# Four small row loads of an attention stage issued from ScalarE's queue instead of SyncE's

## The chip, the cores and the metric

The kernel runs on one core of a Trainium2 chip. The metric is the time of one execution on the device in microseconds (us). The five engines of the core run side by side, each through its own list of instructions in order: TensorE (PE; its weight loads are shown as PEld), VectorE (DVE), ScalarE (ACT), GpSimd (POOL) and SyncE (SP). SP issues nearly all transfers (DMA); ACT can issue transfers too, between its own instructions.

## The reference

Attention over 4 batches of 8 heads, with a causal mask and a bias from the running sum of `s`; its output goes through two gated MLPs (called MoE).

```python
# q, k, v: (4, 8, 576, 64), s: (4, 8, 576)
scores = (1 / sqrt(64)) * q @ k.T
cum = cumsum(maximum(s, 0), axis=-1)
bias = -(cum[:, :, :, None] - cum[:, :, None, :])
scores = where(causal, -1e9, scores + minimum(bias, 0))
attn = softmax(scores)
x = (attn @ v) as (2304 tokens, 512)
x = rmsnorm(x) * rms_g
x = (silu(x @ w_gate) * (x @ w_val)) @ w_out      # d_ff 1536
x = (silu(x @ w2_gate) * (x @ w2_val)) @ w2_out   # d_ff 1536
```

## The kernel before

The tokens of a batch are cut into group A (queries 0 to 255) and group B (256 to 575). Groups A of batches 0 and 1 are computed first, in a cheaper way, while the first weights still come in: these are the 16 *early heads*, called here head 0 to head 15 in their order (0 to 7 are batch 0, 8 to 15 batch 1; class `EarlyUnit`, function `attend_early`). After them, the norm of group A of batch 0 (`normalise`) and the first gate and value matmuls of the MoE (`moe1`, L1086) run; the later attention heads lie between those.

For an early head the scores are one matmul per query tile (`scores`, L899; two tiles: "first" and "second" scores), in float32, with 128 rows to contract: 64 of q and k, and one row more, row `D`, that holds 1 on the q side and the cumulated s on the k side, so that the matmul adds the cumulated s. The rest is zero. Both sides lie in a tile `lq` (two tiles, `lq_117` and `lq_121`, each with two halves, so head n uses the place of head n - 4). DVE adds the mask and finds the extremum of a row (L690), ACT takes the exponential (L701), PE transposes it (L917), ACT or DVE copies the result out (`pTA`, L922 or L923), PE multiplies with v (L927, the "values"), and ACT or DVE copies into `x` (L932 or L933). The squares of `x` for the norm are summed by tiny matmuls (L965, 128x2). The first step on PE from the norm towards the MoE is a transpose at L1058; L1066 and L1086 follow.

The method `load` issues an early head's transfers: q and k (L879, 128 KB), for heads 4 to 15 the row of the cumulated s (L884, `lq<-cumA`, 1 KB, from a tile in SBUF to row `D` of `lq`), and v (L891, 64 KB; for the first four heads from ACT, L888). The weights of the first MLP are loaded in pieces of 512 KB (L434, `raw<-in_w_gv`); ACT and DVE and POOL turn them into two float32r parts (L438 to L449).

What stands where is set by a planner (`Plan`): every piece of work is told to it with an engine, an estimated duration and a priority (`pri`, the lower the sooner), and it plays the engines against an inner clock and writes their lists in the order that comes out. For a transfer, SP's entry is free for the next after 450 ns at least, while what reads the data is due some 2.3 us later; `later` is a further delay that it adds between what the transfer waits for and its issue. Work of an early head has priority n on the compute engines, its transfers n - 1000. On the chip the lists are fixed, and semaphores make each instruction wait for what it needs. The transfers take eight semaphores (DMAHW0 to DMAHW7) in turn, and each waits until the transfer before it on its own semaphore has landed.

Of the kernel before, what the change touches and what calls it, by code (L numbers as in the profile page):

```python
# [22 lines left out]
NB, NH, S, D = 4, 8, 576, 64  # L23
# [17 lines left out]
PE, DVE, ACT, POOL, SP, NONE = "PE", "DVE", "ACT", "POOL", "SP", "NONE"  # L41
# [38 lines left out]
class Plan:  # L80
# [20 lines left out]
    def op(self, eng, ns, fn, r=(), w=(), pri=0.0, later=0, port=False, slow=0.0):  # L101

        n = len(self.ops)
        done = 0
        if eng == SP:  # L110
            took = ns / self.RATE
            ns = max(450.0, took)
            done = 2300.0 + took - ns + slow
        deps, shared = set(), []
        for accesses, writes in ((r, False), (w, True)):
            for a in accesses:
                buf, part = a if isinstance(a, tuple) else (a, None)
                key = buf if isinstance(buf, str) else buf.key
                live = self.live.setdefault(key, [])
                keep = []  # L120
                for part2, m, wrote in live:
                    meets = part is None or part2 is None or part == part2
                    if meets and (writes or wrote) and m != n:
                        deps.add(m)
                    if not (writes and meets and (part is None or part == part2)):
                        keep.append((part2, m, wrote))
                keep.append((part, n, writes))
                self.live[key] = keep
                if not isinstance(buf, str) and buf.share is not None and buf not in shared:
                    shared.append(buf)  # L130
                    buf.uses += 1
        engs = eng if isinstance(eng, list) else [(eng, ns)]
        self.ops.append((engs, fn, deps, pri, done, shared, later, port))
        return n
# [166 lines left out]
def tile_kernel(  # L301
# [16 lines left out]
    op = plan.op  # L318
# [10 lines left out]
    def buf(pool, tag, shape, dtype, name=None):  # L329
        return Buf(f"{pool}.{tag}",  # L330
                   lambda: pools[pool][1].tile(shape, dtype, name=name or tag, tag=tag))
# [143 lines left out]
    cumA = buf("at", "pTB1", [P, 2 * P], F32, "cumA")  # L475
# [100 lines left out]
    class Head:  # L576
# [13 lines left out]
        def load(self, pri):  # L590
            b, h, n, nv = self.b, self.h, self.n, self.nv
            i = b * NH + h
            c0 = self.c0
            q0, k0, c0_ = lq_parts(self.ql, 0)
            q1, k1, c1_ = lq_parts(self.ql, 1)
            self.qp, self.kp = [k0, k1], [q0, q1, c0_, c1_]
            op(SP, 4 * P * n, lambda en: en.dma_start(
                out=self.ql()[:, :n], in_=qk[b, h, :, 1, :n]), w=self.kp, pri=pri, later=2500)
            op(SP, 4 * D * (QW - c0), lambda en: en.dma_start(
                out=self.ql()[:D, S + c0:], in_=qk[b, h, :D, 0, c0:]),  # L600
               w=self.qp, pri=pri, later=2500)
            op(SP, 4 * P * n, lambda en: en.dma_start(
                out=self.cb()[:, :n], in_=cum_d[i:i + 1, :n].to_broadcast([P, n])),
               r=["cum_d"], w=[self.cb], pri=pri, later=2500)
            op(SP, 256 * P * nv, lambda en: en.dma_start(out=self.vl()[:, :nv], in_=vp[b, h, :, :nv]),
               w=[self.vl], pri=pri, later=2500)
# [241 lines left out]
    class EarlyUnit(Unit):  # L848
# [28 lines left out]
        def load(self, pri):  # L877
            ql, i = self.ql
            op(SP, 8 * D * 256, lambda en: en.dma_start(  # L879
                out=ql()[0:D, :, 288 * i:288 * i + 256], in_=qk[self.b, self.h, 0:D, :, 0:256]),  # L880
               w=self.parts[:2], pri=pri)
            n = self.b * NH + self.h
            if not self.first:
                op(SP, 1024, lambda en: en.dma_start(  # L884
                    out=ql()[D:D + 1, 1, 288 * i:288 * i + 256], in_=cumA()[n:n + 1]),
                   r=[cumA, self.rows], w=self.parts[2:], pri=pri, later=1000)
            if self.first:
                op(ACT, 450, lambda en: en.dma_start(  # L888
                    out=self.v(), in_=vp[self.b, self.h, :, 0:2]), w=[self.vl], pri=pri - 1e6)
            else:  # L890
                op(SP, 512 * P, lambda en: en.dma_start(  # L891
                    out=self.v(), in_=vp[self.b, self.h, :, 0:2]), w=[self.vl], pri=pri)
# [241 lines left out]
    later = setup()  # L1134
# [767 lines left out]
```

## Time and profile before

| | us |
|---|---|
| median of 3 timed runs (lowest, highest) | 1055.18 (1053.97, 1057.35) |
| the profiled execution | 1057.39 |
| its span, first to last instruction of the program | 1055.6 |
| PE busy in the span | 1040.2 (99%) |
| DVE, ACT, POOL busy | 771.7, 641.5, 273.5 |
| mean granted clock of PE, share of full speed | 0.997 |

The profiled execution's own time is 1.8 us more than its span: that lies before the first and after the last instruction. A busy PE in the profile says that matmuls are under way, and not at which rate; the granted clock, at one of two levels (1.00 is 2.4 GHz, 0.50 is 1.2 GHz), is told for each stretch.

### The profile page before, as it was taken

What the parts mean: (1) busy time and instruction counts of PE and PEld (TensorE: products, weight loads), DVE (VectorE), ACT (ScalarE), POOL (GpSimd) and SP (SyncE); (2) the same over time, 40 slices, a digit from 0 to 9 for tenths busy, and PEclk for the clock granted to TensorE, in tenths of its full rate; (3) what the DMA queues carried; (4) which work ended last, traced back from release to release, by engine and by line L of the source; (5) the groups of instructions that cost most, each with busy time, mean ns of one, the idle gap of its engine ahead of it and who ended that gap; (6) DMA issues with size and microseconds to landing.
All of it is one profiled execution on the core that took longest, in us unless ns stands there. A gap on an engine that the chain in (4) does not pass through costs nothing.

```text
span 1055.6 us, 19496 instructions
## 1 busy us (share of the span) xinstructions
PE 1040.2 (99%) x6322; PEld 937.2 (89%) x6322; DVE 771.7 (73%) x1880; ACT 641.5 (61%) x1373; POOL 273.5 (26%) x370
## 2 busy tenths in 40 slices
PE   8899999999999999999999999999999999999998
PEld 6599999999999999999988889888888888888888
DVE  7699788777777776757779887665667766976462
ACT  6689778867664775333466865555556444665652
POOL 4368556544343542000000000212122221300000
PEclk9899999999999999999999999999999999999999
DMA  7797555534546732666697662666667667888673
GB/s 204 229 282 221 144 150 148 164 117 128 158 142 204 246 106 85 188 208 206 206 299 244 197 222 84 222 210 220 228 202 256 219 232 263 292 259 261 207 244 105
DMA packets 127959, 211.17 MB, mean 200 GB/s; under 512 B 16176, under 2 KB 55600, under 8 KB 127856
## 3 DMA queue, kind: packets, MB, share of 16 engines
q1 hardware_dynamic: 126656, 209.32, 62.8%
q8 instruction: 50, 0.82, 0.3%
q10 hardware_dynamic: 1200, 0.60, 0.2%
q14 instruction: 53, 0.43, 0.1%
HBM read 145.29 MB, written 64.56 MB: 199 GB/s over the span
## 4 chain that ended last, share of the span: by engine, by line
PE 79%; DMA 7%; DVE 6%; ACT 3%; issue 3%; POOL 1%; SPq 1%; ACTq 0%; POOLq 0%; DVEq 0%
PE mo L1086 21%; PE mo L1455 8%; PE mo L1626 8%; PE sps L1626 6%; PE tp L1455 6%; PE sps L1455 5%; PE tp L745 4%; PE tp L733 3%; PE sps L664 2%; PE mo L1702 2%; DMA raw<-in_w_gv 2%; PE sps L1086 2%; PE tp L1086 2%; PE mo L1510 2%; DMA lq<-cumA 1%
## 5 line engine op out<-in xcount | busy, mean ns | idle before, releaser
L1086 PE MATMUL mo<-xL,H 128*128 128x256 f32 (+1 forms) x672 | 201.8, 300 | 0.1
L1086 PE MATMUL mo<-xH,H 128*128 128x256 f32 (+1 forms) x672 | 200.7, 300 | 0.3
L1086 PE MATMUL mo<-xH,L 128*128 128x256 f32 (+1 forms) x672 | 200.2, 298 | 0.0
L1351 DVE TENSOR_TENSOR hL<-hh,hH 128x512 fp32r<-128x512 f32 (+1 forms) x192 | 125.2, 662 | 67.1 <-ACT hH L1348 66.4
L1348 ACT ACTIVATE hH<-hh 128x512 fp32r<-128x512 f32 (+1 forms) x192 | 115.2, 603 | 91.6 <-DVE hL L1351 21.3
L1086 PEld LDWEIGHTS mo<-xL,H 128*128 128x128 f32 x672 | 127.0, 189 | 1.0 <-POOL xL L1075 0.5
L1086 PEld LDWEIGHTS mo<-xH,H 128*128 128x128 f32 x672 | 126.7, 189 | 1.1 <-ACT xH L1073 0.6
L1086 PEld LDWEIGHTS mo<-xH,L 128*128 128x128 f32 x672 | 126.9, 189 | 0.2
L701 ACT ACTIVATE sc<-sc,col 128x128 f32<-128x128 f32 (+3 forms) x128 | 73.2, 572 | 48.4 <-DVE col L690 46.1
L1455 PE MATMUL mo<-hH,wo 128*128 128x512 f32 x312 | 97.8, 389 | 0.0
L1455 PEld LDWEIGHTS mo<-hH,wo 128*128 128x128 f32 x312 | 58.6, 188 | 12.2
L1455 PE MATMUL mo<-hL,wo 128*128 128x512 f32 x156 | 61.1, 391 | 0.2 <-DVE hL L1351 0.2
L1455 PE MATMUL tp<-hH,wo 128*128 128x512 f32 x192 | 60.4, 389 | 0.0
L1093 ACT ACTIVATE t<-mo 128x256 f32<-128x256 f32 (+1 forms) x84 | 33.9, 403 | 43.4 <-PE mo L1086 43.3
L1632 ACT ACTIVATE u<-sps 128x512 f32<-128x512 f32 x48 | 28.5, 593 | 50.6 <-PE sps L1626 48.8
L745 PE MATMUL tp<-pTB,vst 128*128 128x320 f32 (+2 forms) x320 | 52.2, 294 | 1.6 <-ACT pTB L736 1.0
L1455 PE MATMUL sps<-hH,wo 128*128 128x512 f32 x168 | 52.9, 389 | 0.0
L1095 DVE SCALAR_TENSOR_TENSOR t<-t,mo 128x256 f32<-128x256 f32 (+1 forms) x84 | 37.8, 450 | 19.4 <-ACT t L1093 19.1
L738 DVE TENSOR_TENSOR pTB<-tp,pTB 128x512 fp32r<-128x512 f32 x64 | 44.0, 687 | 8.3 <-ACT pTB L736 7.2
L745 PEld LDWEIGHTS tp<-pTB,vst 128*128 128x128 f32 x320 | 46.5, 189 | 3.6 <-ACT pTB L736 1.7
L1589 POOL TENSOR_TENSOR tmp<-x,x 128x512 f32<-128x512 f32 x2 | 2.9, 1454 | 178.5 <-DVE x L1471 178.5
L733 PE MATMUL tp<-ident,sc 128*128 128x128 f32 x304 | 46.9, 274 | 0.6 <-DVE x L754 0.4
(289 smaller groups left out, 2925.9 us busy)
## 6 DMA issues: line engine op xcount, KB each, us to landing
raw<-in_w_gv SPq DMA_DIRECT2D x44, 511.8 KB, 5.4
tb<-h_d SPq DMA_DIRECT2D x48, 256.0 KB, 3.9
t<-tb SPq DMA_DIRECT2D x48, 256.0 KB, 2.4
hh<-t SPq DMA_DIRECT2D x48, 256.0 KB, 3.1
lq<-in_qk SPq DMA_DIRECT2D x32, 288.0 KB, 3.6
cb<-cum_d SPq DMA_DIRECT2D x32, 288.0 KB, 3.9
hh<-h_d SPq DMA_DIRECT2D x36, 256.0 KB, 3.6
h_d<-hh SPq DMA_DIRECT2D x54, 128.0 KB, 2.3
```

Of the source, the lines that this page charges most:

```text
L701: op(ACT, c_act(o + m, 2) + 35, lambda en: en.activation(sc()[:m, :o + m], sc()[:m, :o + m], ACTF.Exp, scale=-1.0, bias=col()[:m, 0, t:t + 1],
L733: op(PE, C_TR, lambda en, pt=pt, a=a, kb=kb, t=t: en.transpose(pt()[:, a * P:a * P + P], self.sc[t]()[:, kb * P:kb * P + P], ident()), r=[ ...
L738: op(DVE, c_tt(n), lambda en, pt=pt, c=c: en.tensor_tensor(out=place(L, c), in0=source(pt, c), in1=f32(place(H, c)), op=ALU.subtract), r=[ ...
L745: op(PE, c_mm(n), lambda en, w=w, z=z, kb=kb, d0=d0, n=n, o=o: en.matmul(po()[:, o:o + n], vst[j]()[:, kb, :], pT[g][z]()[:, d0:d0 + n], s ...
L1086: op(PE, c_mm(n), lambda en, a=a, x=x, c=c, k=k, i=i: en.matmul(ps()[:, :n], a()[:, c], x()[:, k, :n], start=(k == 0 and i == 0), stop=(k ...
L1093: op(ACT, c_act(n), lambda en: en.activation(t()[:, :n], gp()[:, :n], ACTF.Tanh, scale=0.5), r=[gp], w=[t], pri=pri)
L1095: op(DVE, c_tt(n), lambda en: en.scalar_tensor_tensor(out=t()[:, :n], in0=t()[:, :n], scalar=1.0, in1=gp()[:, :n], op0=ALU.add, op1=ALU.mu ...
L1348: op(ACT, c_act(n) + 35, lambda en: en.activation(H(), src(), ACTF.Copy), r=[src, *after], w=[H], pri=pri)
L1351: lambda en: en.tensor_tensor(out=L(), in0=src(), in1=f32(H()), op=ALU.subtract),
L1455: op(PE, c_mm(n), lambda en, m=m, w=w, xx=xx, kk=kk, i=i: en.matmul(ps[m]()[:, :n], w(), xx(), start=first and kk == 0 and i == 0, stop=kk ...
L1626: op(PE, c_mm(n), lambda en, w=w, xx=xx, cut=cut, kk=kk, i=i: en.matmul(ps()[:, :n], W[w]()[:, cut], xx(), start=first and kk == 0 and i == 0,
L1632: op(ACT, c_act(n), lambda en: en.activation(dst(), ps()[:, :n], ACTF.Copy), r=[ps], w=[dst], pri=-1.0e4)
```

## The change

For heads 12 to 15, the row of the cumulated s is issued from ACT's queue and not from SP's. The planner is told 450 ns on ACT, the delay `later` of 1000 is taken out, and the priority of the issue is n - 3 among ACT's other work (n - 1000 before, on SP). Heads 4 to 11 keep their rows on SP. What is transferred stays the same.

```diff
             n = self.b * NH + self.h
             if not self.first:
-                op(SP, 1024, lambda en: en.dma_start(
+                late = self.i >= 2 * NH - 4
+                op(ACT if late else SP, 450 if late else 1024, lambda en: en.dma_start(
                     out=ql()[D:D + 1, 1, 288 * i:288 * i + 256], in_=cumA()[n:n + 1]),
-                   r=[cumA, self.rows], w=self.parts[2:], pri=pri, later=1000)
+                   r=[cumA, self.rows], w=self.parts[2:], pri=pri + 997 if late else pri,
+                   later=0 if late else 1000)
```

Since the planner orders all engines together, the lists differ from there on. The lines behind the edit shift by two: L899 becomes L901, L891 L893, and so on.

On SP, before: the list from the q and k of head 12 on to the q and k of head 14. `lq1_121` holds the odd heads, `lq0_117` the even ones; `raw` is a weight load, `vl` a v load (heads 10, 11 and 12 here); the semaphores that an entry waits for stand in brackets.

```order
L879 DMA lq0_117<-in_qk 64x2x256 [waits DMAHW6_49,PE_49]
L891 DMA vl0_126<-in_vp 128x128 [waits DMAHW7_49,PE_49]
L884 DMA lq0_117<-cumA_114 1x16x16 [waits DMAHW0_49]
L434 DMA raw0_455<-in_w_gv 128x2047 [waits DMAHW1_49]
L891 DMA vl1_136<-in_vp 128x128 [waits DMAHW2_49,PE_49]
L434 DMA raw1_479<-in_w_gv 128x2047 [waits DMAHW3_49]
L879 DMA lq1_121<-in_qk 64x2x256 [waits DMAHW4_49]
L891 DMA vl0_126<-in_vp 128x128 [waits DMAHW5_49,PE_49]
L884 DMA lq1_121<-cumA_114 1x16x16 [waits DMAHW6_49]
L879 DMA lq0_117<-in_qk 64x2x256 [waits DMAHW7_49]
```

The same place on SP now.

```order
L879 DMA lq0_117<-in_qk 64x2x256 [waits DMAHW0_49,PE_49]
L893 DMA vl0_126<-in_vp 128x128 [waits DMAHW1_49,PE_49]
L434 DMA raw0_451<-in_w_gv 128x2047 [waits DMAHW2_49]
L434 DMA raw1_470<-in_w_gv 128x2047 [waits DMAHW3_49]
L893 DMA vl1_136<-in_vp 128x128 [waits DMAHW6_49,PE_49]
L879 DMA lq1_121<-in_qk 64x2x256 [waits DMAHW7_49,DMAHW5_49]
L879 DMA lq0_117<-in_qk 64x2x256 [waits DMAHW0_49,PE_49]
```

The rows are gone from SP, and the second weight load stands one entry sooner; the q and k of head 13 still stand behind both weight loads. The v load of head 10 now waits for DMAHW1.

On ACT, the list now, from the exponential of head 8's second scores on to the copy of head 9's transposes (before, the same list without the four DMA entries, except for numbers).

```order
L701 ACTIVATE sc10_427,tot1_149<-sc10_427,col0_186 128x256 [waits DVE_49]
L885 DMA lq0_117<-cumA_114 1x16x16 [waits DMAHW1_49,PE_49,Pool_49]
L924 ACTIVATE pTA1_260<-tp0_436 128x384 [waits PE_49]
L701 ACTIVATE sc01_449,tot1_149<-sc01_449,col1_201 128x128 [waits DVE_49,Activation_49]
L885 DMA lq1_121<-cumA_114 1x16x16 [waits DMAHW6_49,DMAHW5_49,PE_49]
L438 ACTIVATE cvy_173<-raw1_379 128x512 [waits DMAHW0_49]
L701 ACTIVATE sc11_464,tot1_149<-sc11_464,col1_201 128x256 [waits DVE_49,Activation_49]
L960 ACTIVATE sq1_110<-x0_119 128x256 [waits DVE_49]
L924 ACTIVATE pTA0_223<-tp0_468 128x384 [waits PE_49]
L701 ACTIVATE sc00_478,tot1_149<-sc00_478,col2_217 128x128 [waits DVE_49]
L701 ACTIVATE sc10_485,tot1_149<-sc10_485,col2_217 128x256 [waits DVE_49,Activation_49]
L885 DMA lq0_117<-cumA_114 1x16x16 [waits DMAHW3_49,DMAHW4_49,PE_49,Pool_49]
```

The row of head 12 stands behind head 8's exponential, on the semaphore DMAHW1 that the v load on SP waits for; head 13's follows two entries on, head 14's (the last entry shown) and head 15's, right behind it, stand ahead of the copy of head 9's transposes.

On PE, before: from the second scores of head 12 to the second scores of head 13. The values of head 10 (`tp1_548`) and the transposes of head 11 (`tp0_557`) stand ahead of the first scores of head 13 (`sps0_564`).

```order
L899 MATMUL sps1_537<-lq0_117 128x256
L927 MATMUL tp1_548<-pTA0_223,vl0_126 64x256
L927 MATMUL tp1_548<-pTA0_223,vl0_126 64x128
L917 MATMUL tp0_557<-ident_140,sc01_510 128x128
L917 MATMUL tp0_557<-ident_140,sc11_515 128x128 x2
L899 MATMUL sps0_564<-lq1_121 128x128
L965 MATMUL mo2_569<-half_228,sq0_334 128x2 x2
L899 MATMUL sps1_575<-lq1_121 128x256
```

The same place on PE now.

```order
L901 MATMUL sps1_541<-lq0_117 128x256
L901 MATMUL sps0_551<-lq1_121 128x128
L929 MATMUL tp1_558<-pTA0_223,vl0_126 64x256
L929 MATMUL tp1_558<-pTA0_223,vl0_126 64x128
L919 MATMUL tp0_564<-ident_140,sc01_517 128x128
L919 MATMUL tp0_564<-ident_140,sc11_521 128x128 x2
L901 MATMUL sps1_571<-lq1_121 128x256
```

The first scores of head 13 have moved ahead of head 10's values and head 11's transposes. Some 25 rows further on, the transpose at L1060 (L1058 before) stands behind the values of head 14 and the transposes of head 15, which before stood behind it.

## Rows read from the trace of the kernel before

**Rows 1.** The page, busy us (share of the span) and instructions of each engine.

```profile
PE 1040.2 (99%) x6322; PEld 937.2 (89%) x6322; DVE 771.7 (73%) x1880; ACT 641.5 (61%) x1373; POOL 273.5 (26%) x370
```

**Rows 2.** Stretches: length, busy PE, PEld, DVE, ACT, POOL, granted clock, DMA share, GB/s.

```profile
10.00:20.00 10.00, 8.74 (x52) 6.04 (x50) 7.23 (x29) 8.60 (x26) 4.69 (x8) 1.00 0.64 162
...
20.00:30.00 10.00, 9.90 (x61) 6.94 (x60) 8.48 (x31) 9.15 (x30) 4.78 (x5) 1.00 0.70 186
...
35.83:38.31 2.48, 0.00 (x1) 0.03 (x1) 0.60 (x2) 1.22 (x3) 1.45 (x2) 0.99 0.67 205
38.31:45.00 6.69, 6.69 (x21) 4.47 (x22) 2.67 (x12) 1.98 (x8) 1.94 (x2) 0.50 0.53 153
...
60.00:1040.00 980.00, 975.94 (x5934) 886.52 (x5934) 723.87 (x1714) 595.97 (x1244) 250.24 (x332) 1.00 0.63 201
```

**Rows 3.** Waits of PE, 0 to 60 us: us in total, times, longest.

```profile
PE sps L899 <- DMA lq<-cumA: 3.5, 2, 2.5
```

**Rows 4.** Chain that ended last, 5 to 52 us: start, us, what.

```profile
31.70 6.48 DMA lq<-cumA
```

**Rows 5.** Timeline of PE: start, us, instruction, count, idle before it.

```profile
14.07 0.46 PE L899 MATMUL sps<-lq 128*128 128x128 f32 x2 [1.05 <-DMA lq<-cumA]
...
33.68 0.60 PE L899 MATMUL sps<-lq 128*128 128x256 f32 x2
34.49 0.86 PE L927 MATMUL tp<-pTA,vl 128*64 128x256 f32 x4 [0.21 <-ACT pTA L922]
35.28 0.55 PE L917 MATMUL tp<-ident,sc 128*128 128x128 f32 x3
38.31 0.77 PE L899 MATMUL sps<-lq 128*128 128x128 f32 x2 [2.48 <-DMA lq<-cumA]
```

**Rows 6.** Timeline of SP's queue: start, us, transfer issued.

```profile
25.96 0.54 SPq L879 DMA_DIRECT2D lq<-in_qk  x1
26.60 1.56 SPq L891 DMA_DIRECT2D vl<-in_vp  x1
28.21 0.55 SPq L884 DMA_DIRECT2D lq<-cumA  x1
28.82 0.57 SPq L434 DMA_DIRECT2D raw<-in_w_gv  x1
...
29.91 0.43 SPq L434 DMA_DIRECT2D raw<-in_w_gv  x1
30.38 0.55 SPq L879 DMA_DIRECT2D lq<-in_qk  x1
```

**Rows 7.** Issues near 30.4 and 28.2 us, KB, us to landing; all twelve rows.

```profile
lq<-in_qk SPq DMA_DIRECT2D x1, 128.0 KB, 7.3
...
lq<-cumA SPq DMA_DIRECT2D x1, 1.0 KB, 1.8
...
DMA to landing us min/median/max: 1.7/4.8/7.4
```

**Rows 8.** Timeline of ACT: start, us, instruction, idle before it.

```profile
1.17 2.28 ACTq L888 DMA_DIRECT2D vl<-in_vp  x4
...
26.15 0.19 ACT L701 ACTIVATION_READ_ACCUMULATOR sc<-sc,col 128x1 f32 x1
26.50 0.49 ACT L922 ACTIVATE pTA<-tp 128x384 f32<-128x384 f32 x1 [0.17 <-PE tp L917]
...
31.87 0.49 ACT L922 ACTIVATE pTA<-tp 128x384 f32<-128x384 f32 x1 [0.87 <-PE tp L917]
```

**Rows 9.** Timeline of PE, from head 13's values to the MoE.

```profile
46.68 0.86 PE L927 MATMUL tp<-pTA,vl 128*64 128x256 f32 x4 [0.65 <-DVE pTA L923]
...
48.52 0.38 PE L1058 MATMUL mo<-ident,sq 128*128 128x128 f32 x2
48.83 0.86 PE L927 MATMUL tp<-pTA,vl 128*64 128x256 f32 x4
...
52.31 0.44 PE L917 MATMUL tp<-ident,sc 128*128 128x128 f32 x2 [0.49 <-ACT sc L701]
```

## The prediction

> **What bounds the kernel now.** I read the busy totals first: TensorE (PE) is busy 1040.2 of 1055.6 us [rows 1], so whatever the change is worth must show as PE idle time, or as PE time at the lower clock. The stretches [rows 2] say where that is. From 60 to 1040 us PE stands idle only 980 - 975.94 = 4.06 us; the change's own place, the early heads before 52.6 us, is where PE waits. There the list of PE's waits has one row at its head: the scores matmul waits 3.5 us, in two pieces, the longest 2.5, for `lq<-cumA`, the row of the cumulated s [rows 3]. The timeline of PE shows them: 1.05 us at 14.07 (head 4, which the change leaves alone) and 2.48 us, 35.83 to 38.31, ahead of the scores of head 13 [rows 5]. Right behind the second the granted clock goes to 0.50, the lower level (1.2 GHz), from 38.31 to 45, with PE busy all of the 6.69 us [rows 2]. The same work at the higher level would take half, so the fall costs up to 3.35 us.
>
> The chain of waits names the transfer: the row of head 13 is issued at 31.70 and lands 6.48 us later, at 38.18 [rows 4]; the matmul follows 0.13 us behind. But the same matmul needs head 13's q and k too, and these were issued on the same queue at 30.38 and took 7.3 us [rows 6, 7]: they landed at 37.68. So of the 2.48 us, only the last 0.50 belong to the row; the other 1.98 belong to q/k, which stand behind two weight loads of 512 KB each (28.82 and 29.91) [rows 6].
>
> **The change, term by term.** Times are those of the profiled execution, 1057.39 us in all, of which the span is 1055.6 and 1.8 lies around it. It stands 2.21 us above the median of the three timed runs (1055.18), so the terms are summed first and then put on the median.
>
> *Rows leave SP's queue.* Four issues of 0.55 us go. Only the row of head 12 (28.21) stands ahead of q/k of head 13; the next entry, a weight load, started 0.61 us after it [rows 6]. So q/k come 0.61 us earlier (if nothing new holds SP, below) and land at 37.07. The row of head 13, issued on ACT near 28 us and not at 31.70, lands long before; its 0.50 us is gone. Together: PE resumes 0.50 + 0.61 = 1.11 us earlier, at 37.20. **-1.11.**
>
> At this place a rule speaks against the change. The twelve rows, 1.0 KB each, landed from SP's queue in as little as 1.7 and as much as 7.4 us [rows 7]: what is queued ahead decides, not the size. The Trainium skill ("DMA: Bandwidth & Descriptors", section "Issuing engines are not separate DMA queues") says that transfers issued from several engines share the same 16 DMA engines and that only the time of the issuing sequencer is saved. By that alone the sum would lose the 0.50 and keep the 0.61, which ends at 1055.9. No run here yet shows a small row on ACT's queue next to heavy SP traffic.
>
> *Work that PE now does behind the wait.* The order shows head 13's first scores moved ahead of the values of head 10 and the transposes of head 11. Before, these ran from 34.49 to 35.83 [rows 5], ahead of the wait; now PE comes to the wait that much earlier and has them still to do. **+1.34** (at the higher clock).
>
> *Issues on ACT.* Four issues on ACT took 2.28 us, 0.57 each [rows 8]. ACT is busy 9.15 of 10 us from 20 to 30 us [rows 2], so the first two (heads 12 and 13, near 26.3 and 28 us) push its exponentials and copies back by up to 1.14 us, and PE's transposes and values with them. The other two stand ahead of the copy at 31.87, for which ACT sat idle 0.87 us [rows 8]: they hide, but for 0.27. What covers the delay is PE's wait for q/k of head 13: PE would come to it at 35.83 - 1.34 = 34.49, wait until 37.20, which is 2.71 us, and arriving 1.14 later changes nothing. **0**; without that wait, +1.14 to +1.41.
>
> *The clock.* A wait of 2.71 us is nearest to the one of 2.48 that the fall followed. **0**; -3.35 if the clock holds.
>
> *Up to the MoE.* In 46.0 to 52.6 us PE idled 0.65 and 0.49 us [rows 9]. The order now puts L1060 (before: L1058, 48.52), the first PE step of the way from the norm to the MoE, behind the values of head 14 and the transposes of head 15, which before filled waits on that way: they are worth the same 1.34. Bounds -1.14 (both idles gone) to +1.34; the eight small squares matmuls still fill, so I take **0**.
>
> *Everything later.* The planner orders all engines anew after 28 us. The nearest row for what that can do is the idle of 60 to 1040 us, 4.06: gone, or twice as much. **0**, bounds -4.06 to +4.06.
>
> Sum: -1.11 + 1.34 = +0.23. On the profiled time 1057.6, on the median **1055.4 us**.
>
> **Rivals.**
>
> *The clock holds (faster).* If ACT's issues do delay PE by 1.14, the wait at head 13 is 2.71 - 1.14 = 1.57 us, and that is nearer to the 1.05 at 14.07, behind which the granted clock stayed at 1.00 [rows 2], than to 2.48. Then 1055.4 - 3.35 = 1052.1, a hair from the bound of faster. For it: the arithmetic above. Against it: q/k may well land as late as before, which gives 2.2. And the three timed runs spread from 1053.97 to 1057.35, 3.4 us, as much as the fall costs: some of them may not have had it, and then less is to be gained on the median.
>
> *SP is held by a row on ACT (slower).* The transfers take eight semaphores in turn over both queues, and each waits for the transfer before it on its own. In the new order the v load of head 10 on SP (26.60 before) waits for the semaphore of head 12's row on ACT. ACT reaches that row at 26.33 [rows 8]. With the 1.8 us that this row took before [rows 7] it lands at 28.1, and SP's issue of v lasted until 28.16 anyhow [rows 6]: free. With the median of such rows, 4.8 [rows 7], it lands at 31.13, the weight loads go at 31.5 and not 28.21, and q/k of head 13 come 3.3 us later: 1058.7. It decides for slower (over 1058.35) from a landing of about 4.5 us on. For it: half of the twelve rows on SP took 4.8 us or more. Against it: ACT's queue is empty at that time.
>
> *Only the transfer is earlier.* If PE is held by ACT before the wait anyway, the 1.34 is not lost and only -1.11 remains: 1054.1, no change that counts.
>
> *The later order decides.* 1055.4 - 4.06 = 1051.3, or 1059.5.
>
> **How the numbers follow.** 0.3% is 3.2 us, about what a measurement of this kernel can tell from no change: faster is under 1052.0, slower over 1058.3. The forecast has 0.40 (its own range 1053.5 to 1058.0; 0.37 same, 0.03 slower). The clock holds: 0.28 (0.19 faster with any small gain besides, 0.09 same). SP held: 0.14 (all slower but 0.03). Only the transfer: 0.12, same. Later order: 0.06, half each way. Faster 0.19 + 0.03 = 0.22; slower 0.03 + 0.11 + 0.03 = 0.17; same 0.61. The range is that of the later order's two ends, 1051.3 to 1059.5; it takes in the clock's 1052.1 and SP's 1058.7 and leaves out waits on SP near the longest landing of 7.4.
>
> **What would show it.** Right: PE's wait ahead of the scores of head 13 is put down to `lq<-in_qk`, not to `lq<-cumA`, and still lasts 2 to 3 us, ending near 37.2; the rows on ACT's queue land within some 2 us; a stretch at 0.50 follows. Wrong: no row at 0.50 after 38 us (then the clock's rival); SP's v load of head 10 waits beyond 28.5 us (SP held); the wait of head 13 gone altogether, which would say that q/k were not what stood behind the row; or an idle of PE between 60 and 1040 us that is over a microsecond off 4.06.

## The result and the profile after

The changed kernel took 1065.72 us (median of 6 runs, 1063.97 to 1067.12), the kernel before 1056.05 in the runs beside it (6 runs, 1053.0 to 1057.93): a ratio of 1.0103, 95% interval 1.0085 to 1.0121. It is slower by some 10 us. The forecast was 1055.4, no change, with a range that ended at 1059.5: wrong on both counts.

The profiled execution took 1063.97 us, its span 1062.1, 6.5 more than before. On the page (busy us of each engine) PE did the same number of matmuls in 1.9 us more [rows 1], and stood idle 20.0 us (1062.1 - 1042.1) instead of 15.4; DVE is busy 11.8 us longer, POOL 11.0 us less.

```profile
PE 1042.1 (98%) x6322; PEld 938.0 (88%) x6322; DVE 783.5 (74%) x1887; ACT 644.0 (61%) x1378; POOL 262.5 (25%) x358
```

In the stretches that answer to [rows 2] (length, busy PE, PEld, DVE, ACT, POOL, granted clock, DMA share, GB/s) the 2.48 us in which PE stood still ahead of head 13 are now 1.83 us of work, the stretch at the lower clock behind head 13 is gone and one from 50.31 to 60.55 has come, and from 60 to 1040 us PE idles 980 - 972.07 = 7.93 us instead of 4.06.

```profile
35.83:38.31 2.48, 1.83 (x11) 1.16 (x10) 1.78 (x7) 2.43 (x10) 1.50 (x2) 1.00 1.08 236
50.31:60.55 10.24, 10.10 (x42) 9.14 (x43) 8.78 (x20) 8.01 (x18) 5.49 (x6) 0.50 0.82 233
60.00:1040.00 980.00, 972.07 (x5915) 881.60 (x5915) 734.41 (x1718) 594.98 (x1242) 236.16 (x317) 1.00 0.63 200
```

Where the time went is read from equal stretches of both kernels, PE alone (length, PE busy, granted clock, DMA share, GB/s). Before:

```profile
10.00:20.00 10.00, 8.74 (x52) 1.00 0.64 162
...
30.00:40.00 10.00, 7.31 (x38) 0.91 0.84 244
40.00:50.00 10.00, 9.35 (x40) 0.74 0.70 235
50.00:60.00 10.00, 9.51 (x74) 1.00 0.92 290
60.00:70.00 10.00, 10.00 (x80) 1.00 0.91 290
70.00:80.00 10.00, 9.52 (x74) 1.00 0.94 295
...
100.00:1040.00 940.00, 936.59 (x5628) 1.00 0.63 199
```

After:

```profile
10.00:20.00 10.00, 8.39 (x40) 0.83 0.67 167
...
30.00:40.00 10.00, 8.93 (x50) 1.00 0.89 261
40.00:50.00 10.00, 7.02 (x41) 1.00 0.85 251
50.00:60.00 10.00, 9.61 (x40) 0.52 0.87 249
60.00:70.00 10.00, 8.64 (x64) 0.97 0.95 282
70.00:80.00 10.00, 8.56 (x69) 1.00 1.03 342
...
100.00:1040.00 940.00, 934.88 (x5624) 1.00 0.63 199
160.00:200.00 40.00, 38.51 (x296) 1.00 0.47 137
```

Busy time times granted clock is, roughly, the work that PE did at its full rate. From 30 to 40 us the changed kernel did 2.3 us more of it (8.93 against 7.31 x 0.91 = 6.65): the stall of head 13 is gone, as the change intends. From 40 to 80 us it did 7.02 + 9.61 x 0.52 + 8.64 x 0.97 + 8.56 = 29.0 us, the kernel before 9.35 x 0.74 + 9.51 + 10.00 + 9.52 = 36.0. So 7 us are lost in these 40 us, which the change's rows don't touch. From 100 to 1040 us only 1.7 more are, nearly all of it from 160 to 200 us, where PE idles 1.49 us (0.08 before).

Part of the difference between these two traces has nothing to do with the change. In the changed kernel's trace the clock was at 0.50 from 16.18 to 19.59 us as well, behind a wait of 1.61 us for head 4's row. The lists of both kernels are the same there, and the same product with V starts at 25.12 us before and at 27.19 after: 2.1 of the 6.5 us of span were there before the first moved row was issued. Of the 20 traces of this case seven have a fall between 14 and 21 us, among them s2 and h3, which follow the list of the kernel before there; so it comes and goes from execution to execution.

PE's timeline (start, us, instruction, idle before it) shows what is left of the wait at head 13, a new wait of 2.76 us ahead of head 14's product with V, and the first MoE matmul (L1088) at 54.42.

```profile
37.76 0.46 PE L901 MATMUL sps<-lq 128*128 128x128 f32 x2 [0.65 <-DVE col L690]
...
44.95 0.55 PE L919 MATMUL tp<-ident,sc 128*128 128x128 f32 x3
48.26 0.86 PE L929 MATMUL tp<-pTA,vl 128*64 128x256 f32 x4 [2.76 <-ACT pTA L924]
...
50.25 1.51 PE L929 MATMUL tp<-pTA,vl 128*64 128x256 f32 x4 [0.43 <-DVE pTA L925]
...
54.42 0.76 PE L1088 MATMUL mo<-xH,H 128*128 128x256 f32 x2
```

In the kernel before the first MoE matmul stood at 51.24:

```profile
51.24 0.57 PE L1086 MATMUL mo<-xH,H 128*128 128x256 f32 x2
```

ACT's timeline says what the copy pTA waited for: it stands behind two weight conversions (L438, `cvy<-raw`), and ACT idled 1.05 us in front of the second for a weight that had not landed, then did head 15's exponentials.

```profile
43.87 0.76 ACT L438 ACTIVATE cvy<-raw 128x512 f16<-128x512 bf16 x1
45.69 0.77 ACT L438 ACTIVATE cvy<-raw 128x512 f16<-128x512 bf16 x1 [1.05 <-DMA raw<-in_w_gv]
46.34 0.37 ACT L701 ACTIVATE sc<-sc,col 128x128 f32<-128x128 f32 x1
...
47.74 0.47 ACT L924 ACTIVATE pTA<-tp 128x384 f32<-128x384 f32 x1
```

The rows themselves: ACT spent 2.25 us on four issues; they landed 2.3, 1.7, 5.6 and 6.0 us later. In SP's waits, v loads stood 2.9 us for rows.

```profile
27.88 0.61 ACTq L885 DMA_DIRECT2D lq<-cumA  x1
...
33.53 0.63 ACTq L885 DMA_DIRECT2D lq<-cumA  x1
```

```profile
SPq L893 <- DMA lq<-cumA: 2.9, 2, 1.4
```

So SP's timeline has the v load of head 10 at 30.20 and q/k of heads 13 and 14 from 32.06.

```profile
30.20 0.33 SPq L893 DMA_DIRECT2D vl<-in_vp  x1
...
32.06 1.19 SPq L879 DMA_DIRECT2D lq<-in_qk  x2
```

### The profile page after: what moved, and what is told of

Read it like the earlier page. It is cut to its first block, busy times and chain, and to the rows that moved or that the text cites. A ratio compares the mean times of both kernels' runs of the same rounds, so it can differ in the third digit from the quotient of the medians.

```text
span 1062.1 us, 19485 instructions
## 1 busy us (share of the span) xinstructions
PE 1042.1 (98%) x6322; PEld 938.0 (88%) x6322; DVE 783.5 (74%) x1887; ACT 644.0 (61%) x1378; POOL 262.5 (25%) x358
## 4 chain that ended last, share of the span: by engine, by line
PE 79%; DVE 6%; DMA 4%; ACT 2%; issue 2%; SPq 0%; POOL 0%; ACTq 0%; DVEq 0%
PE mo L1088 19%; PE mo L1628 10%; PE sps L1628 8%; PE mo L1457 8%; PE sps L1457 5%; PE tp L1457 5%; PE tp L745 4%; PE mo L1704 3%; PE tp L733 3%; PE sps L664 2%; PE sps L1088 2%; PE tp L1088 2%; PE mo L1512 2%; PE tp L1628 1%; DMA tb<-h_d 1%
## 5 line engine op out<-in xcount | busy, mean ns | idle before, releaser
L1088 PE MATMUL mo<-xL,H 128*128 128x256 f32 (+1 forms) x672 | 201.4, 300 | 0.5 <-DVE xL L1077 0.3
L1088 PE MATMUL mo<-xH,H 128*128 128x256 f32 (+1 forms) x672 | 200.5, 300 | 0.2
L1088 PE MATMUL mo<-xH,L 128*128 128x256 f32 (+1 forms) x672 | 199.9, 298 | 0.0
L1088 PEld LDWEIGHTS mo<-xL,H 128*128 128x128 f32 x672 | 127.4, 190 | 1.6 <-DVE xL L1077 0.8
L1088 PEld LDWEIGHTS mo<-xH,H 128*128 128x128 f32 x672 | 127.0, 190 | 1.1 <-issue 0.3
L1088 PEld LDWEIGHTS mo<-xH,L 128*128 128x128 f32 x672 | 127.3, 190 | 0.2
L1634 ACT ACTIVATE u<-sps 128x512 f32<-128x512 f32 x48 | 28.5, 594 | 53.6 <-PE sps L1628 53.6
L1643 ACT ACTIVATE u<-u 128x512 f32<-128x512 f32 x48 | 29.6, 631 | 29.8 <-DVE u L1638 29.7
```

The lines of the kernel that those rows point to most:

```text
L1088: op(PE, c_mm(n), lambda en, a=a, x=x, c=c, k=k, i=i: en.matmul(ps()[:, :n], a()[:, c], x()[:, k, :n], start=(k == 0 and i == 0), stop=(k ...
```

## The experiments

Three theories stood at the start: the new order of all the other work costs it (O), the issue of rows on ACT and the hold of SP cost it (I), the clock's fall comes by chance (C). For each run three numbers are given behind the median: the ratio to the kernel before on the same chip with its interval, and the mean over the runs of the *lost clock*, which is span x (1 - mean granted clock) of each run, to about 1 us since the clock is listed to 0.001. For the kernel before it is 3.1 us (85 runs beside the experiments, mean time 1055.9), for the changed kernel 7.6 (6 runs, mean 1065.5). Time less lost clock is then 1052.9 and 1057.9: of the 9.6 us, 4.6 are clock and 5.0 are not.

### The issue alone, the order alone

`e1_issue_only`: the kernel before, its plan untouched; only the call goes to ACT's queue.

```
-                op(SP, 1024, lambda en: en.dma_start(
+                op(SP, 1024, lambda en: (nc.scalar if self.i >= 2 * NH - 4 else en).dma_start(
```

> The order of the kernel before on every engine, word for word; only the four rows of heads 12 to 15 leave SP's queue and stand on ACT's at the places where the old order had them. Theory O (the 10 us come from the new order of the other work: two weight conversions now stand on ACT ahead of head 14's copy of P, and ACT waits in front of them for a weight that SP issued late): about 1055 us, within 4 of the kernel before, and no PE wait above 1 us between 40 and 60 us that ends with ACT's copy of P. Theory I (the issue of the rows on ACT itself, 2.2 us of ACT and SP held by their semaphores for 2.9 us, costs it): 1061 to 1066 us. Theory C (the clock's fall came by chance and hangs on neither): about 1055 in most runs, 1061 in some.

`e2_order_only`: the changed kernel, its plan untouched; only the call goes to SP's queue.

```
-                op(ACT if late else SP, 450 if late else 1024, lambda en: en.dma_start(
+                op(ACT if late else SP, 450 if late else 1024, lambda en: nc.sync.dma_start(
```

> The order of the changed kernel on every engine; only the four rows are issued by SP, at the places of that order, and ACT issues none. Theory O: 1062 to 1068 us, with a PE wait of 2 to 3 us near 48 us that ends with ACT's copy of P, and a stretch at the granted clock 0.5 behind it. Theory I: 1054 to 1058 us, the wait near 48 us under 1 us.

e1: 1058.28 us, 1.0017 [0.9991, 1.0044], lost clock 5.1, the rest 1052.7. e2: 1065.36 us, 1.0101 [1.0056, 1.0145], lost clock 7.5, the rest 1057.9: the changed kernel's figures, part by part. PE's stretches of e1 repeat those of before:

```profile
40.00:50.00 10.00, 9.35 (x39) 0.73 0.76 246
50.00:60.00 10.00, 9.51 (x72) 1.00 0.93 301
```

Those of e2 those of after, here with 31.6 us of work from 40 to 80:

```profile
40.00:50.00 10.00, 7.97 (x46) 1.00 0.89 276
50.00:60.00 10.00, 8.28 (x41) 0.68 0.85 238
60.00:70.00 10.00, 9.10 (x71) 0.98 0.97 301
70.00:80.00 10.00, 9.10 (x73) 1.00 1.02 329
```

The trace of e2 is the better one to compare with the kernel before, since the clock did not fall at head 4 in it: the product that starts at 25.12 us before starts at 25.01. Its first MoE matmul comes 2.0 us later than before, and of its span, 5.7 us longer, 4.4 are lost from 40 to 80 us and 2.6 from 100 to 1040 us (1.4 of them from 160 to 200); some is gained earlier.

```profile
53.19 0.48 PE L1088 MATMUL mo<-xH,H 128*128 128x256 f32 x2 [1.06 <-POOL kLL L619]
```

Theory I falls: without a single row on ACT the loss is whole, and what the rows on ACT cost in the old order is not told from nothing. The interval of e1 leaves room for 4.6 us; half of its ten runs took 1059 us or more, at a clock of 0.991 to 0.995, and on the mean it is 1.6 us above the runs beside it with 1.8 us more lost clock. Theory C falls as the whole cause too, since each run of e2 and of the changed kernel lies above all 85 of the kernel before (the longest took 1062.93). Theory O stands.

### One instruction, one wait, one row

`e4_conv_behind` moves the second conversion behind the copy, on ACT alone (in the list that is issued, the instruction is taken out and put behind the copy).

```
         out.sort()
+        seq = [o for o in out[:at[dst] + 1] if o[2] not in moved]
+        out = seq + [o for o in out[:at[dst] + 1] if o[2] in moved] + out[at[dst] + 1:]
```

> The changed kernel with one instruction moved on ACT: the conversion of the weight whose load it waited for 1.05 us (the second of the two ahead of head 15's exponentials) stands behind head 14's copy of P; the order on the other engines is that of the changed kernel. Theory O in its narrow form (that conversion in front of the copy makes the 2.76 us wait, and the wait makes the clock fall): the PE wait near 48 us is 0.9 to 1.5 us (2.76 less the 1.05 and the 0.77 of the conversion), the stretch at 0.5 behind it shrinks or goes, 1056 to 1062 us. Theory I: 1064 to 1066 us, with the clock's fall still at 50 us.

1065.0 us, 1.0087 [1.0051, 1.0124], lost clock 6.0. The wait shrank to 0.99 us, as worked out, and the time did not follow. PE's timeline of this kernel shows it waiting 2.72 us a little later, at the first MoE matmul. The row names POOL's `kLL`, which ended at the same moment; what that matmul reads is `xH`, which ACT began at 54.12, behind a conversion that had itself waited 1.55 us for its weight, a copy for the next attention, one of head 15 and a weight part.

```profile
46.86 0.86 PE L941 MATMUL tp<-pTA,vl 128*64 128x256 f32 x4 [0.99 <-ACT pTA L936]
...
54.63 0.77 PE L1100 MATMUL mo<-xH,H 128*128 128x256 f32 x2 [2.72 <-POOL kLL L629]
```

The narrow form of theory O falls: that wait is not the loss, only the place where it showed.

`f1_after_fill` and `f2_before_fill` let PE work where it waits: nine matmuls whose output is overwritten.

```
-                op(PE, 0.422 * 4 * n, lambda en, kb=kb, o=o, d0=d0, n=n: en.matmul(
+                op(PE, 0.422 * 4 * n, lambda en, kb=kb, o=o, d0=d0, n=n: [en.matmul(
+                    po()[:, :P], ident(), ident(), start=True, stop=True)
+                    for _ in range(9 if self.i == 14 and kb == 0 else 0)] and None or en.matmul(
```

In f2 they stand ahead of head 13's scores, in the bank of these scores, with this condition:

```
+                    for _ in range(9 if self.i == 13 and t == self.tiles[0] else 0)] and None or en.matmul(
```

> The changed kernel with nine idle matmuls (128x128 of ident, written to head 14's own PSUM bank and overwritten by its product) issued by PE ahead of head 14's product with V, where PE waited 2.76 us; no other instruction moves. Theory K (the loss is mainly TensorE at 1.2 GHz from 50.31 to 60.55, in the first MoE matmuls, and the clock fell because PE had little to do from 45.5 to 48.3): the clock holds, 4 to 5 us come back (10.24 us at half clock is 5.1 us of work), 1060 to 1062 us. Theory W (the MoE's start waits for weights and for ACT anyway, so the clock there costs nothing): the clock holds or not, 1064 to 1067 us.

> The kernel before with nine such matmuls ahead of head 13's scores, where PE waited 2.48 us for head 13's row; no other instruction moves. If the half clock from 38.28 to 45.11 costs PE its 3.4 us, as the prediction put it, and the clock holds: 1051.5 to 1053 us. If the chain through ACT and DVE sets the pace of the last early heads (the other kernels, at full clock there, did only 1 us more of PE's work from 40 to 50): 1054.5 to 1056 us. If the fall only moves to the start of the MoE: 1058 to 1060 us.

f1: 1067.6 us, 1.0108 [1.007, 1.0146], lost clock 7.5, as without them. In the profiled execution the clock still fell, at 56.88 us, 5.4 us behind head 14's product and the waits there (2.05 in the changed kernel), and for 6.83 us and not 10.24; its other falls stand at 16, 340 and 569 us, so the lost clock of a run is not the MoE's alone. Theory K is not borne out, and not refuted either, since the clock never held. f2: 1054.89 us, 0.9995 [0.9977, 1.0012], lost clock 1.6. Here it did hold in the profiled execution, where the nine (2.17 us, two passes each) stand in the place of the wait:

```profile
35.53 2.17 PE L899 MATMUL sps<-ident 128*128 128x128 f32 x18
37.54 0.39 PE L901 MATMUL sps<-lq 128*128 128x128 f32 x2
```

On the mean the runs are 0.3 us shorter than those beside them with 0.5 us less lost clock (against all 85 runs of the kernel before 1.2 and 1.5), which the interval doesn't separate from nothing. That is a mean over executions with and without a fall. What one fall costs is read from two traces with the same order: from head 13's first scores to the first MoE matmul PE took 51.24 - 38.31 = 12.93 us with the fall and 47.30 - 37.54 = 9.76 without, 3.2 us less, about the 3.35 of the prediction.

```profile
47.30 0.58 PE L1088 MATMUL mo<-xH,H 128*128 128x256 f32 x2
```

`g1_before_fill2` adds five ahead of head 4's scores.

```
-                    for _ in range(9 if self.i == 13 and t == self.tiles[0] else 0)] and None or en.matmul(
+                    for _ in range({4: 5, 13: 9}.get(self.i, 0) if t == self.tiles[0] else 0)] and None or en.matmul(
```

> The kernel before with idle matmuls where PE waits for a row: five ahead of head 4's scores and nine ahead of head 13's. If the falls of the clock that these waits bring cost what they take (the runs of the kernel before lost 3.0 us of granted clock on the mean, and their times rise by 1.1 us for each): 1.5 to 2.5 us faster than the kernel before. If they fall at other places instead: within 1 us.

1055.68 us, 0.9992 [0.9972, 1.0012], lost clock 1.4: no further gain, since the rest is 1054.7, 1.8 us more than in the kernel before. `f3_e3_fill` has such fills at three places of the kernel e3 (below).

```
+                    for _ in range(4 if self.i == 14 and kb == 0 else 0)] and None or en.matmul(
...
+                for _ in range(2 if not split and i == 0 and k == 0 else 0)] and None or en.matmul(
...
+                    for _ in range(3 if go else 0)] and None or en.matmul(
```

> The kernel whose planner was told later weights (rows on ACT, 1061 us), with idle matmuls where its PE waited: four ahead of head 14's product (1.02 us), two ahead of the first sum of the norm (0.45), three ahead of the first matmul of the MoE (0.69). Theory K: no fall of the clock at 51.8, 3.4 us come back, 1057 to 1058.5 us. Theory W: 1060 to 1062 us.

1066.47 us, 1.0098 [1.0059, 1.0137], lost clock 4.0 where e3 has 4.1, and the rest rose by 4.8 us. In the profiled execution the clock did hold at the start of the MoE, as theory K wanted (1.00 from 22 to 100 us; it fell at 14 us, behind head 4, ahead of all fills; in e3's trace it was 0.66 on the mean from 50 to 60), and yet that execution took 1068.28 us. Neither theory had that.

`e3_slow_weights` keeps the change and tells the planner that the early weights land later.

```
-           slow=0.0 if early is None or early > P_ATT - 986 else 1500.0)
+           slow=0.0 if early is None else 3000.0 if early < P_ATT - 980 else 0.0)
```

> The change, rows on ACT three heads ahead; the planner is told 3 us more (instead of 1.5 or 0) for the landing of the early weights, and then writes nearly the order of the kernel before, with head 14's exponentials and copies ahead of the conversions of those weights. Theory O: 1053 to 1058 us, no PE wait over 1 us between 42 and 60 us. Theory I: 1061 to 1066 us, as the rows are issued on ACT as in the changed kernel.

1061.16 us, 1.0055 [1.0029, 1.0081], lost clock 4.1, the rest 1057.1. The planner did not write nearly the old order, as the expectation says, but a third one; so this doesn't part theory O from I, it only shows that a third order is slower too. `d_i15` is the change for one row.

```
-                late = self.i >= 2 * NH - 4
+                late = self.i >= 15
```

> The change for head 15's row alone; the planner writes a third order with it. If three heads of rows on ACT are needed for the loss: within 3 us of the kernel before. If any new order of the work around the end of the early heads loses, by where PE runs dry and the clock falls: 1058 to 1064 us, with a stretch at 0.5 between 45 and 62 us in place of the one at 38 us.

1069.71 us, 1.0141 [1.0107, 1.0175], lost clock 8.3: the largest ratio of all runs here, with one row moved instead of four. In its trace the loss is mostly at another place. PE's stretch there (as above):

```profile
80.00:90.00 10.00, 9.00 (x68) 1.00 0.61 211
90.00:100.00 10.00, 7.39 (x38) 0.66 0.47 129
```

So the size of the loss doesn't go with the size of the change, only with what order the planner draws.

### Which part of the order

Both orders are computed in one kernel; the first part is issued by one, all that is left by the other (MoE + 25 is 25 us of the plan's own time behind its first MoE matmul).

```
+        done = {o[2] for o in one[:k]}
+        seq = one[:k] + [o for o in two if o[2] not in done]
```

> Both orders are worked out; the instructions that the kernel before issues ahead of its first MoE matmul are issued in its order (rows on SP), all that is left behind them in the order of the changed kernel. Theory E (the loss is laid down ahead of the MoE, by the order of heads 12 to 15, the norm and the conversions): 1053 to 1058 us. Theory M (it is laid down in the first 25 us of the MoE, by the order of its weights, of the next attention's heads and its loads): 1062 to 1067 us. Theory L (later still): 1062 to 1067 us.

> The other way round: the changed kernel's order (rows on ACT) until its first MoE matmul, the order of the kernel before for all that is left. Theory E: 1062 to 1068 us. Theory M and theory L: 1053 to 1058 us.

> The order of the kernel before until 25 us of the plan behind the first MoE matmul, the changed kernel's order for the rest. Theory E and theory M: 1053 to 1058 us. Theory L: 1062 to 1067 us.

> The changed kernel's order (rows on ACT) until 25 us of the plan behind the first MoE matmul, the order of the kernel before for the rest. Theory E and theory M: 1062 to 1068 us. Theory L: 1053 to 1058 us.

> The order of the kernel before until 65 us of the plan behind the first MoE matmul, the changed kernel's order for the rest. If nothing is lost behind about 110 us, as the two traces show (PE idle from 100 to 1040 us: 3.4 us before, 5.1 after): 1054 to 1058 us. If the later order has a part of its own in the loss: 1059 to 1064 us.

| | first part, up to | rest | median us | ratio [95%] | lost clock, time less it |
|---|---|---|---|---|---|
| h1 | before, MoE | after | 1069.68 | 1.0118 [1.0092, 1.0145] | 8.6, 1061.0 |
| h3 | before, MoE + 25 | after | 1065.19 | 1.0072 [1.005, 1.0093] | 5.8, 1058.8 |
| h5 | before, MoE + 65 | after | 1063.9 | 1.0069 [1.0049, 1.0089] | 2.6, 1060.9 |
| h2 | after, MoE | before | 1059.42 | 1.0042 [1.0023, 1.0062] | 5.9, 1054.2 |
| h4 | after, MoE + 25 | before | 1061.08 | 1.0049 [1.0029, 1.0068] | 7.4, 1054.5 |

None of the theories E, M and L has this pattern. Behind the changed kernel's early part the old order gets most of the 5 us that aren't clock back (h2, h4), so theory E fails as the only cause; the lost clock stays, 5.9 and 7.4 against 3.1, so in these two that part goes with the early order. How the old order gets the rest back the traces don't say: h4's PE idles 21.4 us (1059.5 - 1038.1), no less than the changed kernel's. But h1, h3 and h5 are no clean test of the later order: each loses right behind its own seam, wherever that is. PE's stretches of h3, whose seam comes near 78 us:

```profile
40.00:60.00 20.00, 18.82 (x129) 1.00 0.99 309
...
80.00:100.00 20.00, 17.93 (x113) 0.74 0.40 123
```

and of h5, where PE of the kernel before is busy 40.00 and 39.92 of these 40 us:

```profile
120.00:160.00 40.00, 36.81 (x275) 1.00 0.54 157
160.00:200.00 40.00, 38.62 (x292) 1.00 0.44 130
```

Of h5's two rows only the first is the seam's. The idle time from 160 to 200 us is in every trace that has the changed kernel's later order (1.35 to 1.51 us in that kernel, e2, e4, f1, h1, h3, h5 and s1) and in none of those with the old one (0.08 at most in the kernel before, e1, f2, g1, h2, h4 and s2; the kernels t1 and t2, below, are left out): this much the later order costs by itself. At a seam, what one order had put off and the other taken for done comes in a lump (argued, not tried), so for the rest these three show what a mismatch costs.

h1 against h3 is of use all the same. Where the first MoE matmuls stand in PE's order decides what fills PE between the last early heads. The kernel before has them ahead of head 15's last transposes and its product (h3 keeps that):

```
113 L917 MATMUL tp_683<-ident,sc_652 128x128
114 L1066 MATMUL mo_690<-xL_660,sel 128x256
115 L1086 MATMUL mo_696<-xH_685,H_267 128x256
116 L1086 MATMUL mo_698<-xH_685,H_267 128x256
117 L917 MATMUL tp_683<-ident,sc_656 128x128 x2
118 L1086 MATMUL mo_696<-xL_660,H_267 128x256
```

The changed kernel has all of heads 14 and 15 ahead of them:

```
105 L929 MATMUL tp_666<-pTA_223,vl_126 64x256
...
108 L919 MATMUL tp_679<-ident,sc_641 128x128 x2
...
110 L929 MATMUL tp_694<-pTA_260,vl_136 64x256
...
118 L1088 MATMUL mo_737<-xH_731,H_267 128x256
```

At h1's seam head 15's transposes and product slip ahead of the MoE too. PE's timeline of h1 shows it waiting at just these, and the MoE (L1131) coming behind at half rate, 0.41 us for a matmul that takes 0.28 at the higher clock:

```profile
49.12 0.69 PE L961 MATMUL tp<-ident,sc 128*128 128x128 f32 x2 [1.62 <-ACT sc L741]
50.45 1.54 PE L971 MATMUL tp<-pTA,vl 128*64 128x256 f32 x4 [0.65 <-DVE pTA L967]
51.93 0.80 PE L1131 MATMUL mo<-xH,H 128*128 128x256 f32 x2
...
54.69 0.41 PE L1131 MATMUL mo<-xH,L 128*128 128x256 f32 x1
```

`s1_after_hoist` and `s2_before_hoist` ask whether the norm of the first group, on which the MoE waits, is what comes late.

```
+            start[n] = min(start[n], ready)
+        seq = sorted(seq, key=lambda o: (start[o[2]], o[1]))
```

> The changed kernel with the end of the first group's norm (from the last product on DVE through the transposes, the four sums on PE, the four products and the halves xH and xL) moved up in the order to where its own inputs are ready in the plan: on PE ahead of heads 14's and 15's products, on ACT ahead of the next attention's conversions. SP and POOL keep their order. Theory N (the MoE starts 3 us late, at 54.4 us against 51.2, because the norm stands behind these, and PE has nothing else to do): 1059 to 1062 us, the first MoE matmul at 50 to 52 us. Theory S (the loss is spread over the conversions, the loads and the next heads, and the start of the MoE only shows it): 1064 to 1067 us.

> The same edit to the kernel before. Theory N: the MoE starts up to 1 us earlier, 1053.5 to 1055 us. Theory S: within 2 us of the kernel before, either side.

s1: 1069.14 us, 1.0118 [1.009, 1.0145], lost clock 8.3. The four sums of the norm now end before 47.5 us on PE, and yet the first MoE matmul (L1164) comes at 55.75, later than before the edit, since PE's queue has heads 14 and 15 between them. PE's timeline of s1:

```profile
47.04 0.38 PE L1141 MATMUL mo<-xL,sel 128*128 128x256 f32 x1
49.08 0.86 PE L1001 MATMUL tp<-pTA,vl 128*64 128x256 f32 x4 [1.66 <-ACT pTA L996]
...
52.55 1.54 PE L1001 MATMUL tp<-pTA,vl 128*64 128x256 f32 x4 [2.13 <-DVE pTA L997]
...
55.75 0.56 PE L1164 MATMUL mo<-xH,H 128*128 128x256 f32 x1
```

Theory N falls: it is not the norm. s2: 1058.88 us, 1.0019 [1.0001, 1.0037], slower by 2 us at the edge of the noise, which neither theory expected.

### Which engine

In the new plan some 80 instructions that two engines can do change places between POOL and DVE or ACT.

```
+        other = {o[2]: o[3] for o in two}
+        seq = [(t, i, n, e if n in self.rows else other[n]) for t, i, n, e in seq]
```

> The changed kernel's order, rows on ACT; each instruction that the planner may give to one of two engines goes to the engine that it has in the kernel before. Theory G (the half of the loss that isn't the clock comes from the work that the new plan puts on DVE, 783.5 us against 771.7): DVE busy 770 to 775 us, 1058 to 1062 us, the time less the lost clock at 1053 to 1055. Theory T (it comes from the order in time): 1064 to 1068 us, the time less the lost clock at 1057 to 1061.

> The order of the kernel before, rows on SP, with the engines of the changed kernel. Theory G: DVE busy 780 to 786 us, 1059 to 1062 us, the time less the lost clock at 1057 to 1060. Theory T: 1054 to 1058 us, the time less the lost clock at 1052 to 1055.

t1: 1068.62 us, 1.0132 [1.0097, 1.0167], lost clock 8.3, DVE busy 778.1 us. t2: 1068.6 us, 1.0123 [1.0094, 1.0153], lost clock 2.4, DVE busy 780.8. Both are slower than either whole plan, t2 without any of it being clock. Neither theory holds: order and choice of engine were worked out together, and either half with the other's counterpart loses 13 us.

## Why the prediction was wrong

**The row's 0.50 us, and q/k 0.61 us earlier (-1.11).** Half right. In the profiled execution PE's wait for `lq<-cumA` at head 13 went, and so did the whole wait (0.65 us behind DVE is left at 37.76). But q/k of head 13 were issued at 32.06 and not at 29.8, since SP's v load of head 10 was issued at 30.20, beyond the 28.5 named as the sign of the rival "SP is held by a row on ACT". Its mechanism was real, its price was not: e2, with no row on ACT, loses the same. How long PE waits at head 13 differs from execution to execution: in e2, which has the changed kernel's order, it was 2.56 us, put down to q/k as forecast, and in f1, which has its rows on ACT too, 2.12 us, put down to the row.

**Work behind the wait (+1.34).** The order is as read, but the cost needs the wait. In the profiled execution the wait was gone, and PE did 2.3 us more by 40 us instead of losing 1.34.

**Issues on ACT (0).** Not contradicted: e1 has them in the old order, 1.0017 [0.9991, 1.0044]. The Trainium skill ("DMA: Bandwidth & Descriptors", section "Issuing engines are not separate DMA queues") was put against this change; the landings agree with it, 5.6 and 6.0 us for the two rows on ACT's otherwise empty queue while SP's loads ran, against 4.8 as the median from SP's [rows 7]. It does not bear on the loss, which e2 has with all rows on SP.

**The clock (0, or -3.35 if it holds).** This step failed in its form. It asked whether the fall behind head 13 stays or goes, and gave the going a gain. In the profiled execution it went from there and came at 50.31, for 10.24 us instead of 6.83, at the start of the MoE, where PE is busy 10.10 of 10.24 us and each us at half rate is half a us lost: 5.1. That is no accident of one execution: of the ten traces whose order up to the MoE is the changed kernel's or e3's (edited ones too) nine have a fall between 48 and 64 us, all but f3. The price at head 13 was right (3.2 us between the traces of f2 and of the kernel before); that the same loss could come back a little later, and larger, was in no term. Nor does the length of the wait, by which the rival judged, decide whether the clock falls: behind head 4's wait it fell after 1.61 us in the changed kernel's trace and stayed at 1.00 after 2.51 us in e4's.

**Up to the MoE (0, bounds -1.14 to +1.34), and everything later (0, bounds -4.06 to +4.06).** This is the step that failed: the new order of everything behind head 13 was put at nothing, and it lost 7.0 us of PE's work from 40 to 80 us (4.4 in e2). "The eight small squares matmuls still fill" was wrong: they stand behind the products and fill nothing, and PE stood 2.76 + 0.43 us where it had stood 0.65 + 0.49. The MoE began 3.2 us later, of which 2.1 were there at 27 us already, by chance; in e2, without that, it began 2.0 us later, beyond the bound of 1.34. And the measure for the later order was badly chosen. The idle of 60 to 1040 us says how well *this* order keeps PE busy, not how far another one may miss it; it came to 7.93, just inside "twice as much" (3.87 against 4.06), but the clock of the early MoE and the wait ahead of it come on top, which no bound had together. "The later order decides" had 0.06; the three other orders that the planner drew (the changed kernel's, also in e2; e3's; d_i15's) and two edits of the first (e4, s1) took 1061 to 1070 us against 1056.

**What is shown, and what is not.** Shown: the loss is the plan's, not the transfers'; in the traces most of it is made from 40 to 80 us, and 1.4 us from 160 to 200; about half of it is TensorE at 1.2 GHz; no single one of the wait, the conversion, the norm and the choice of engines, as tried here, carries it. Argued, from h1, h3 and s1, but not tried: that the changed kernel loses because its PE queue has heads 14 and 15 whole ahead of the first MoE matmul, so that PE waits for ACT's and DVE's copies with no MoE work to fill, where the kernel before has it. The test would be to move the first MoE matmuls ahead of those products in the changed kernel. A rival to it lies on ACT: the first MoE matmul reads `xH`, which ACT begins at 50.73 in the kernel before and at 53.92 in the changed kernel, behind a copy for the next attention that came later before (L612, at 54.71 then and 52.23 now). s1 moved the norm up on both engines at once and does not part the two. Open: why the changed kernel still lacks work from 60 to 80 us, what in f3 cost 5 us, and whether the order before is simply a lucky draw among many, which would make most others slower; no run here tells how orders are spread. No version that beats the kernel before was found; f2 is the nearest, and it is the same within what was measured.

## What to carry to other kernels

Where a planner orders all engines by estimates, an edit of four transfers is an edit of the whole order: first run the edit with the order frozen and the new order without the edit, before any instruction is costed. A wait that is taken away early can let PE run ahead into the next place where it lacks work; look at what stands there in its queue, and for how long the clock would fall there. And an instruction that filled a wait counts as a loss when the new order puts it behind that wait, even if its own result comes in time.

## What the runs showed of the hardware

The runs of one and the same kernel spread over 12 us (85 runs of the kernel before, 1050.55 to 1062.93), and the granted clock explains half of the variance: the time rises by 0.94 us for each us of lost clock, with a correlation of 0.72. The 14 runs with a mean clock of 0.999 or 1.000 took 1053.2 us on the mean, the 16 at 0.995 or less 1059.2. The Trainium skill ("TensorE: Matmul & The Clock Gate", section "Terms") puts the penalty of the lower clock at the time spent there times the share of pulses withheld; over these runs that agrees.

A fall of 6.83 us at head 13 cost 3.2 us, about half its length (the traces of f2 and of the kernel before, which have the same order). The length of PE's wait alone does not say whether the clock falls: at head 4 it fell behind a wait of 1.61 us (the changed kernel) and not behind one of 2.51 us (e4).

Idle matmuls in a gap did not do the same everywhere: nine of them in front of head 13's scores, and the clock of that execution stayed at 1.00 (f2); nine in front of head 14's product, and it fell 5.4 us behind that product, at the next waits (f1); nine spread over three places, and it stayed at 1.00 from 22 to 100 us (f3), though the runs were no shorter.
